# Attention with a gated convolution FFN on one core: q, k and v laid out by the host, masks by a matmul, V's level step folded in, a new order

## The chip, the core and the metric

The program runs on one core of a Trainium2 chip: TensorE (PE, with its weight loads PEld), VectorE (DVE), ScalarE (ACT), GpSimd (POOL) and SyncE (SP), which issues most DMAs. The metric is the device time of one execution in microseconds (us); lower is better.

## The reference

Eight batches, eight heads, 576 positions, head size 64. Block-causal attention (blocks of 64) is followed by an FFN with a convolution of three taps and a gate; the FFN's weights come as float64.

```python
scores = scale * np.matmul(q, k.transpose(0, 1, 3, 2))      # scale = 1/8
scores = np.where(block_i >= block_j, scores, -1000000000.0)
attn = np.exp(scores - np.max(scores, axis=-1, keepdims=True))
attn = attn / (np.sum(attn, axis=-1, keepdims=True) + 1e-09)
x = np.matmul(attn, v)                                       # heads side by side: 576 x 512 a batch
h = np.maximum(x @ w_in, 0.0)                                # 512 -> 1024
conv = sum(conv_w[k] * hp[:, k:k + S, :] for k in range(3))  # hp: h with a zero row at each end
out = h * (1 / (1 + np.exp(-conv))) @ w_out                  # 1024 -> 512
```

## The kernel before

The heads are taken in pairs, two heads of 64 on the 128 partitions, 32 pairs in all. Batch 0 (pairs 0 to 3) is worked in two visits a pair, "A" (queries 0 to 255, `stage_sa`) and "B" (the rest, `stage_sb`), while the weights are loaded, decoded from float64 and split. The 28 pairs of batches 1 to 7 are worked in one visit each (`stage_s`), while PE runs the FFN of the batch before: `ffn` has up projections (L1824), the relu, convolution and gate on ACT, DVE and POOL (L1841 to L1877), and down projections (L1910).

Numbers that need more than one pass of PE are kept as a high and a low part: `qh`, `ql`, `kh`, `kl` for q and k, and three matmuls (high x high and the two mixed products) make a product.

**q and k.** `load_nat` (from L718) loads a pair's q and k with the positions on the partitions, head by head, in rows of 256 bytes, and the last 64 positions by themselves (L731). `naturals` (from L1156) transposes them on PE into a PSUM bank, three 128x128 tiles a group (L1166). For a later pair (`stage_t`) there are three groups, nine transposes. Then ACT writes the high part (L1179, for q with the scale 1/8) and DVE subtracts it from the bank to get the low part (L1182), four pieces each. The last 64 queries of the two heads are also copied to the two corners of a 128x128 tile with zeros elsewhere (`qdh`, `qdl`; ACT L1192, DVE L1195), so that one matmul gives both heads' last scores (L1318). In batch 0 the transposes are L1224 (visit A) and L1166 (visit B), evicted by ACT (L709), and the corners are filled by DMAs (L1244).

**Scores of a later pair.** `stage_s` makes them in three visits (L1391, the two heads on the two halves of the rows). ACT then overwrites the masked 64x64 corners of the bank with -1e9 (L1404, six times a pair), DVE takes the maxima (L1413), ACT the exponentials and their sums (L1416), DVE a reciprocal (L1432, L1436). `two_planes` scales the probabilities into two float16 planes (POOL L1271 or ACT L1273 for the first, DVE L1276 for the second: it reads the probabilities and the first plane, both in SBUF), DMA transposes turn them, and `pair_pv` multiplies them with V (L1781). In batch 0 the mask is a matmul already (L1481, L1542): the identity times a tile of -1e9 on 64 rows, added into the bank.

**V of a later pair.** `load_v` loads it in rows of 256 bytes by four to six issues; ACT sums its magnitudes (L809), PE, DVE and POOL make a power of two of them (L812 to L823), POOL scales V by it (`level`, L829), copies it to float16 (`high`, L704) and subtracts (`low`, L835).

**The order.** The function `order` of the class `Plan` merges the five engines' queues; each operation's place on its engine is set by its number in `TARGETS`. PE is filled up where it would idle with matmuls whose result nobody reads (`work`, L2038). PSUM banks are given out in that order too, eight in all.

## Time and profile before

| | us |
|---|---|
| median of 3 runs | 714.97 |
| lowest, highest | 714.72, 715.11 |
| span of the profiled execution | 711.6 |

The profiled execution's span is 3.4 us under the median of the runs; durations below come from it. The page gives, among others, the busy share of each engine over the span. The trace answers by line, by stretch of time and in order of time. Two neighbouring instructions of an engine overlap at their ends in these records, so that what one costs its queue is read from one start to the next.

### The profile page before, as it was taken

To read this page: it belongs to the slowest core of one execution; us is meant where nothing else is said; L and a number is where in the kernel's file an instruction comes from. 1 tells how busy PE (TensorE), PEld (TensorE's weight loads), DVE (VectorE), ACT (ScalarE), POOL (GpSimd) and SP (SyncE) were. 2 spreads that over 40 slices of the span, in tenths; PEclk is the share of its full clock that TensorE was granted. 3 is DMA by queue.
4 is the path that set the end of the run, shared out by engine and by line. 5 is a ranking of instruction groups with operands and counts; after the bars stand their busy time and mean duration, and the time that the engine had idled before them with its cause. 6 is when DMAs were issued, how large, how long until landed. Compare 5 with 4: busy or idle time off the path is not lost.

```text
span 711.6 us, 17406 instructions
## 1 busy us (share of the span) xinstructions
PE 689.4 (97%) x5824; PEld 575.2 (81%) x5824; DVE 600.5 (84%) x1553; ACT 589.8 (83%) x1859; POOL 476.0 (67%) x716
## 2 busy tenths in 40 slices
PE   8899999998999999999999999999899999999998
PEld 6567778777889788887978888897778879888987
DVE  5999989998888979999988898888998888994441
ACT  6889989897979779798979889997888779884753
POOL 2545285665877758778787758877676767775543
PEclk9999999999999999999999999999999999999999
DMA  8845437699667794957866796877877595574001
GB/s 212 249 101 140 127 63 156 133 184 169 135 133 133 132 178 93 187 111 168 129 133 132 127 183 122 156 143 123 155 125 143 106 192 113 102 141 85 17 29 45
DMA packets 313197, 94.35 MB, mean 133 GB/s; under 512 B 302461, under 2 KB 307605, under 8 KB 313109
## 3 DMA queue, kind: packets, MB, share of 16 engines
q1 hardware_dynamic: 307812, 84.47, 62.1%
q10 hardware_dynamic: 5296, 8.78, 3.8%
q8 instruction: 46, 0.75, 0.4%
q14 instruction: 43, 0.34, 0.2%
HBM read 37.38 MB, written 9.44 MB: 66 GB/s over the span
## 4 chain that ended last, share of the span: by engine, by line
PE 56%; DVE 17%; ACT 16%; issue 3%; POOL 3%; SPq 2%; DMA 2%; ACTq 0%; POOLq 0%; DVEq 0%
PE bank L1910 19%; PE bank L1824 17%; PE bank L1391 5%; PE bank L1781 4%; PE bank L1719 3%; DVE ptbl L1276 3%; DVE su L1413 3%; PE bank L1166 2%; PE bank L1318 2%; ACT t L1864 2%; ACT t L1844 2%; DVE t L1848 2%; ACT bank L1841 1%; DVE t L1867 1%; DVE h L1276 1%
## 5 line engine op out<-in xcount | busy, mean ns | idle before, releaser
L1824 PE MATMUL bank<-x,wih 128*128 128x290 f32 (+3 forms) x1024 | 195.0, 302 | 4.0 <-DVE t L1867 1.8
L1824 PEld LDWEIGHTS bank<-x,wih 128*128 128x128 f32 x1024 | 153.6, 188 | 15.2 <-DVE t L1867 4.3
L1877 POOL TENSOR_TENSOR gl<-t,gh 128x289 fp32r<-128x289 f32 (+3 forms) x128 | 107.7, 845 | 43.0 <-ACT gh L1871 36.9
L1910 PE MATMUL bank<-woh,gh 128*128 128x512 f32 (+1 forms) x296 | 120.0, 406 | 0.1
L1910 PE MATMUL bank<-woh,gl 128*128 128x512 f32 (+1 forms) x296 | 114.8, 388 | 0.0
L1910 PE MATMUL bank<-wol,gh 128*128 128x512 f32 (+1 forms) x296 | 114.5, 387 | 0.0
L1824 PE MATMUL bank<-x,wil 128*128 128x290 f32 (+3 forms) x512 | 108.6, 298 | 0.0
L1413 DVE TENSOR_REDUCE su<-bank 128x1 f32<-128x384 f32 (+3 forms) x224 | 101.2, 481 | 6.7 <-ACT bank L1404 5.9
L1848 DVE SCALAR_TENSOR_TENSOR t<-bank,cw,t 128x286 f32<-128x286 f32 (+3 forms) x128 | 65.4, 512 | 21.9 <-ACT t L1844 18.5
L1824 PEld LDWEIGHTS bank<-x,wil 128*128 128x128 f32 x512 | 81.1, 188 | 1.5 <-issue 0.7
L1867 DVE SCALAR_TENSOR_TENSOR t<-t,bank 128x289 f32<-128x289 f32 (+3 forms) x128 | 56.6, 448 | 16.4 <-ACT t L1864 15.1
L1844 ACT ACTIVATE t<-bank,cw 128x287 f32<-128x287 f32 (+3 forms) x128 | 63.6, 499 | 4.7 <-POOL gl L1877 2.2
L1910 PEld LDWEIGHTS bank<-woh,gh 128*128 128x128 f32 x296 | 55.6, 188 | 13.6 <-issue 3.6
L1910 PEld LDWEIGHTS bank<-woh,gl 128*128 128x128 f32 x296 | 55.6, 188 | 12.1
L1864 ACT ACTIVATE t<-t 128x289 f32<-128x289 f32 (+3 forms) x128 | 55.6, 444 | 10.3 <-DVE t L1852 4.8
L1910 PEld LDWEIGHTS bank<-wol,gh 128*128 128x128 f32 x296 | 55.8, 188 | 7.2
L1841 ACT ACTIVATE bank<-bank 128x288 f32<-128x288 f32 (+3 forms) x128 | 51.2, 403 | 9.7 <-PE bank L1824 9.0
L1271 POOL TENSOR_SCALAR ptbl<-p3f,su 128x512 f16<-128x512 f32 x56 | 43.9, 792 | 11.6 <-DVE su L1436 8.3
L1861 POOL TENSOR_TENSOR t<-t,ptah 128x287 f32<-128x287 f32 (+1 forms) x28 | 25.1, 898 | 39.1 <-DVE t L1848 20.9
L1391 PE MATMUL bank<-kh,qh 64*128 64x384 f32 (+3 forms) x224 | 43.7, 375 | 2.8 <-DVE x L1792 1.5
L1276 DVE SCALAR_TENSOR_TENSOR ptbl<-p3f,su,ptbl 128x512 f16<-128x512 f32 x56 | 46.0, 829 | 0.1
L1416 ACT ACTIVATE p3f<-bank,su 128x512 f32<-128x512 f32 x56 | 38.2, 684 | 6.8 <-DVE su L1413 6.6
(206 smaller groups left out, 1864.3 us busy)
## 6 DMA issues: line engine op xcount, KB each, us to landing
out_dram<-stage ACTq DMA_DIRECT2D x33, 256.0 KB, 3.4
vn<-in_v_dram SPq DMA_DIRECT2D x58, 128.0 KB, 2.8
qnf<-in_q_dram SPq DMA_DIRECT2D x56, 128.0 KB, 2.7
knf<-in_k_dram SPq DMA_DIRECT2D x56, 128.0 KB, 2.8
x<-in_moe_w_out_dram SPq DMA_DIRECT2D x8, 512.0 KB, 3.7
gh<-in_moe_w_in_dram SPq DMA_DIRECT2D x4, 512.0 KB, 5.5
gl<-in_moe_w_in_dram SPq DMA_DIRECT2D x4, 512.0 KB, 4.3
qtf<-in_k_dram SPq DMA_DIRECT2D x32, 32.0 KB, 2.6
```

Source lines behind the costliest of these rows:

```text
L1271: nc.gpsimd.tensor_scalar(out=hi(), in0=c(tb.ap), scalar1=st.ap[:, col:col + 1], scalar2=0.0, op0=ALU.mult, op1=ALU.add)
L1276: nc.vector.scalar_tensor_tensor(out=lo(), in0=c(tb.ap), scalar=st.ap[:, col:col + 1], in1=hi(), op0=ALU.mult, op1=ALU.subtract)
L1391: nc.tensor.matmul(home[z][hh].ap[:, cols(i)], t[q_].ap[r, 128 * i:128 * i + 128], t[k_].ap[r, 64 + 128 * (3 - i):S], start=(n == 0), stop ...
L1413: nc.vector.tensor_reduce(out=st.ap[:, k:k + 1], in_=sb.ap[:, cols(i)], op=ALU.max, axis=AX.X, negate=True)
L1824: nc.tensor.matmul(fb.ap[:, 0:n2], wt[:, c, fs], xs[c][xi].ap[:, x0:x0 + n2], start=(n + c - c0 == 0), stop=(n + c - c0 == 3 * NCC - 1))
L1841: nc.scalar.activation(out=fb.ap[:, 0:n2], in_=fb.ap[:, 0:n2], func=AF.Relu, scale=0.5 if b == 0 else 2.0 ** -17)
L1844: nc.scalar.activation(out=t.ap[:, 0:no], in_=fb.ap[:, own:own + no], func=AF.Copy, scale=cw[:, NFC + f:NFC + f + 1])
L1848: nc.vector.scalar_tensor_tensor(out=t.ap[:, i0:no], in0=fb.ap[:, own + i0 - 1:own + no - 1], scalar=cw[:, f:f + 1], in1=t.ap[:, i0:no], o ...
L1864: nc.scalar.activation(out=t.ap[:, 0:no], in_=t.ap[:, 0:no], func=AF.Tanh)
L1867: nc.vector.scalar_tensor_tensor(out=t.ap[:, 0:no], in0=t.ap[:, 0:no], scalar=1.0, in1=fb.ap[:, own:own + no], op0=ALU.add, op1=ALU.mult)
L1877: nc.gpsimd.tensor_tensor(out=gbuf[1].ap[:, f, carry:carry + no], in0=t.ap[:, 0:no], in1=gbuf[0].ap[:, f, carry:carry + no], op=ALU.subtract)
L1910: nc.tensor.matmul(fb.ap[:, 0:cut], gbuf[a].ap[:, f, cs], w[:, f, ds], start=(f == 0 and n == 0), stop=(f == NFC - 1 and n == 2))
```

## The change

- The host hands over q and k transposed: a pair's two heads are the 128 rows, the positions the columns. q has 128 columns behind the first 512: the last 64 queries of the first head (rows 0 to 63, zeros below) and those of the second (rows 64 to 127, zeros above), so the corner tile of before comes as columns 512 to 639. k's blocks of batches 1 to 7 come in the order in which `stage_s` takes them. V comes as one row of 640 numbers a partition.
- `load_qk` loads each of q and k with one issue; `load_v` loads V with one.
- The transposes (L1166, L1224), their evictions, the corner copies and their DMAs are gone. A later pair gets its high part by one ACT copy each for q and k, and its low part by one DVE instruction each, from the loaded tile and the high part, written back over the loaded tile (L1051 of the changed kernel). In batch 0 one instruction scales q in place (`scale_q`, on DVE for pair 0 and on POOL otherwise).
- The mask of the later pairs becomes a matmul behind each visit's scores (L1225), as in batch 0.
- V: `level` is gone; `high` scales by the power of two itself (POOL, L759), and `low` becomes a DVE instruction that scales and subtracts (L762).
- `TARGETS` is another list of numbers; which instruction stands where has changed on every engine, throughout the program.

```diff
     def load_v(p, at, part, load_at=None):
...
-            for j in range(2):
-                nc.sync.dma_start(out=vn.ap[:, 0:4, j, :],
-                                  in_=v[b, h0 + j, 0:512, :].rearrange("(c p) d -> p c d", p=P))
-            for r in range(0 if part else 1, 2):
-                nc.sync.dma_start(out=vn.ap[64 * r:64 * r + 64, 4, :, :],
-                                  in_=v[b, h0:h0 + 2, 512:576, :].rearrange("j p d -> p j d"))
+            nc.sync.dma_start(out=vn.ap.rearrange("p c j d -> p (c j d)"), in_=v[b, p % NP])
...
-        def level():
-            nc.gpsimd.tensor_scalar(out=src(), in0=src(), scalar1=sc.ap[:, 2:3], scalar2=0.0, op0=ALU.mult, op1=ALU.add)
-
         def high():
-            pool_copy(piece(0), src())
+            nc.gpsimd.tensor_scalar(out=piece(0), in0=src(), scalar1=sc.ap[:, 2:3], scalar2=0.0, op0=ALU.mult, op1=ALU.add)
 
         def low():
-            nc.gpsimd.tensor_tensor(out=piece(1), in0=src(), in1=piece(0), op=ALU.subtract)
+            nc.vector.scalar_tensor_tensor(out=piece(1), in0=src(), scalar=sc.ap[:, 2:3], in1=piece(0), op0=ALU.mult,
+                                           op1=ALU.subtract)
...
     def stage_t(nat, at):
-        t = {nm: two([P, S], F32R, nm) for nm in ("qh", "ql", "kh", "kl")}
...
+        (xq, lq), (xk, lk) = nat
+        t = {"ql": xq, "kl": xk, "qh": two([P, QW], F32R, "qh"), "kh": two([P, S], F32R, "kh")}
...
+            def ev_hi(hi=hi, lo=lo, scale=scale):
+                nc.scalar.activation(out=hi.ap, in_=lo.ap, func=AF.Copy, scale=scale)
+
+            def ev_lo(hi=hi, lo=lo, scale=scale):
+                nc.vector.scalar_tensor_tensor(out=lo.raw, in0=lo.ap, scalar=scale, in1=hi.ap.bitcast(F32), op0=ALU.mult,
+                                               op1=ALU.subtract)
...
+                    tiles = GROUP[z]
+                    for hh in range(2):
+                        r = slice(64 * hh, 64 * hh + 64)
+                        x = home[z][hh].ap[0:64, 0:128 * len(tiles)].rearrange("p (j c) -> p j c", c=128)[:, :, 64:128]
+                        nc.tensor.matmul(x, rident[r, r], maskt[r, :].unsqueeze(1).broadcast_to([64, len(tiles), 64]), start=False,
+                                         stop=True, skip_group_check=True)
...
-                    def mk(sb=sb, tiles=tiles):
...
-                            nc.scalar.activation(out=x, in_=maskt[0:64, :].unsqueeze(1).broadcast_to([64, len(tiles), 64]), func=AF.Copy)
...
-                        e = pl.op(DVE, c_dve(128 * i + 128), mx, t0 + 0.3 + OSH * hh, deps=[m], bufs=[sb, st])
+                        e = pl.op(DVE, c_dve(128 * i + 128), mx, t0 + 0.3 + OSH * hh, deps=[o], bufs=[sb, st])
...
 TARGETS = """
-3 1 4 5 14 15 0 2 6 7 8 9 13 12 29 30 18 24 24 26 28 39 42 12 33 51 1 1 0 0 20 17 3 3 6 1 4 0 3 2 5 4 5 1 2 3 4 10 8 6
...
```

PE's queue at the scores of a later pair, in the middle of the program. Names: `dg` belongs to V's power of two, `rident` is the identity, `qnr` a loaded q; L1166 are transposes, L1824 (L1650 after) up projections, L1910 (L1736 after) down projections, L1391 (L1219 after) scores, L1225 masks; `kxr`, `qxr` are the low parts in the loaded tiles. Before:

```order
L815 MATMUL bank<-dg,ones 128x128
L1824 MATMUL bank<-x,wih 128x290 x2
L1166 MATMUL bank<-rident,qnr_110 128x128 x3
L1824 MATMUL bank<-x,wil 128x290 x2
L1824 MATMUL bank<-x,wih 128x290 x4
L1391 MATMUL bank<-kh,qh 128x512 x2
L1391 MATMUL bank<-kl,qh 128x512 x2
L1391 MATMUL bank<-kh,ql 128x512 x2
```

After:

```order
L1736 MATMUL bank<-woh,gl 128x512
L1219 MATMUL bank<-kh,qh 128x128 x2
L1219 MATMUL bank<-kxr_114,qh 128x128 x2
L1219 MATMUL bank<-kh,qxr_110 128x128 x2
L1219 MATMUL bank<-kh,qh 128x256 x2
L1219 MATMUL bank<-kxr_114,qh 128x256 x2
L1219 MATMUL bank<-kh,qxr_110 128x256 x2
L1225 MATMUL bank<-maskt,rident 64x2x64 x2
L1219 MATMUL bank<-kh,qh 128x384 x2
L1219 MATMUL bank<-kxr_114,qh 128x384 x2
L1219 MATMUL bank<-kh,qxr_110 128x384 x2
L1225 MATMUL bank<-maskt,rident 64x64 x2
```

The transposes that stood between the FFN's matmuls are gone, and a mask row closes each visit's scores.

DVE's queue in the same part of the program, where the low parts of q and k are made (L1182 before, L1051 after; L1413 and L1239 are maxima, L1276 and L1104 second planes, L1867 and L1693 the gate's product). Before:

```order
L1182 SCALAR_TENSOR_TENSOR ql<-bank,qh 128x384
L1848 SCALAR_TENSOR_TENSOR t<-bank,cw,t 128x286
L1852 SCALAR_TENSOR_TENSOR t<-bank,cw,t 128x287
L1436 RECIPROCAL su_169<-su_169 128x2
L1182 SCALAR_TENSOR_TENSOR kl<-bank,kh 128x192
L1346 TENSOR_REDUCE su_169<-st_161 128x1
L1867 SCALAR_TENSOR_TENSOR t<-t,bank 128x287
L818 TENSOR_REDUCE vs<-bank 128x1
L1182 SCALAR_TENSOR_TENSOR ql<-bank,qh 128x128
L1182 SCALAR_TENSOR_TENSOR kl<-bank,kh 128x384
```

After:

```order
L1104 SCALAR_TENSOR_TENSOR ptbl<-p1f_95,su_155,ptbl 128x2x128
L1051 SCALAR_TENSOR_TENSOR qxr_112<-qxf_111,qh 128x640
L1104 SCALAR_TENSOR_TENSOR ptbl<-p1f_97,su_155,ptbl 128x2x128
L1174 TENSOR_REDUCE su_155<-st_147 128x1
L1258 TENSOR_SCALAR su_155<-su_155 128x3
L1262 RECIPROCAL su_155<-su_155 128x3
L1051 SCALAR_TENSOR_TENSOR kxr_116<-kxf_115,kh 128x576
L1104 SCALAR_TENSOR_TENSOR ptbl<-p2f_101,su_155,ptbl 128x3x128
```

Four short pieces that read a bank, spread among the FFN's instructions, have become two long ones that read `qxf`, `kxf` and `qh`, `kh` in SBUF.

PE's queue at the start of the program (`blank`, `rident` with 512 columns: fillers; `qkr`: q and k of batch 0 as loaded; L1224 transposes, L1538 and L1364 scores, L1542 and L1368 masks). Before:

```order
L2038 MATMUL bank_177<-blank_145 128x512 x10
L1224 MATMUL bank_201<-rident_132,qkr10_124 128x128 x2
L1224 MATMUL bank_208<-rident_132,qkr00_121 128x128 x2
L1224 MATMUL bank_213<-rident_132,qkr01_122 128x128 x2
L1538 MATMUL bank_216<-kh_206,qh_211 128x128
L1538 MATMUL bank_218<-kh_206,qh_211 128x128
L1542 MATMUL bank_216<-maskt_136,rident_132 64x64
L1542 MATMUL bank_218<-maskt_136,rident_132 64x64
```

After:

```order
L1863 MATMUL bank_161<-blank_135 128x512 x8
L1364 MATMUL bank_183<-kh_170,qh_172 128x128
L1364 MATMUL bank_185<-kh_170,qh_172 128x128
L1368 MATMUL bank_183<-maskt_126,rident_122 64x64
L1368 MATMUL bank_185<-maskt_126,rident_122 64x64
L1364 MATMUL bank_183<-kh_170,qh_172 128x256
L1364 MATMUL bank_185<-kh_170,qh_172 128x256
L1368 MATMUL bank_183<-maskt_126,rident_122 64x64
```

The three groups of transposes ahead of the first scores are gone, and two fillers fewer stand ahead of these. In the whole program 39 fillers have become 31.

## Rows read from the trace of the kernel before

**Rows 1.** Page, section 1: busy time of each engine, share of the span, instructions.

```profile
PE 689.4 (97%) x5824; PEld 575.2 (81%) x5824; DVE 600.5 (84%) x1553; ACT 589.8 (83%) x1859; POOL 476.0 (67%) x716
```

**Rows 2.** Busy us (instructions) in stretches: length, then PE, PEld, DVE, ACT, POOL, clock, DMA.

```profile
36.00:114.00 78.00, 77.61 (x503) 57.54 (x504) 72.95 (x187) 70.54 (x211) 39.09 (x57) 1.00 0.48 115
114.00:690.00 576.00, 561.82 (x5037) 480.93 (x5036) 496.11 (x1276) 482.38 (x1544) 414.06 (x619) 1.00 0.70 133
```

**Rows 3.** PE in order of time, from 321.2 us: start, us, engine, line, operation.

```profile
321.27 0.40 PE L1910 MATMUL bank<-wol,gh 128*128 128x512 f32 x1
321.51 0.39 PE L1910 MATMUL bank<-woh,gl 128*128 128x512 f32 x1
321.74 0.22 PE L1166 MATMUL bank<-rident,qnr 128*128 128x128 f32 x1
321.80 0.23 PE L1166 MATMUL bank<-rident,qtr 128*128 128x128 f32 x1
321.86 0.25 PE L1166 MATMUL bank<-rident,knr 128*128 128x128 f32 x1
321.94 0.46 PE L1910 MATMUL bank<-woh,gh 128*128 128x512 f32 x1
322.25 0.39 PE L1910 MATMUL bank<-wol,gh 128*128 128x512 f32 x1
```

**Rows 4.** Groups by line, weight loads: count, busy us, mean ns, idle before, releasers.

```profile
L1166 PEld LDWEIGHTS bank<-rident,qnr 128*128 128x128 f32 x120 | 14.5, 140 | 5.8 <-DVE t L1867 1.2 <-ACT p2f L1416 0.8 <-DVE x L1792 0.8
L1166 PEld LDWEIGHTS bank<-rident,knr 128*128 128x128 f32 x120 | 13.8, 140 | 5.3 <-ACT p2f L1416 1.4 <-DVE x L1792 0.8 <-DVE ql L1182 0.7
```

**Rows 5.** PE in order of time, from the start: fillers and first masks.

```profile
1.06 4.39 PE L2038 MATMUL bank<-blank 128*128 128x512 f32 x10 [1.06 <-DVE st L593]
...
6.89 0.28 PE L1542 MATMUL bank<-maskt,rident 64*64 64x64 f32 x2
7.00 0.68 PE L1538 MATMUL bank<-kh,qh 64*128 64x256 f32 x4
7.33 0.38 PE L1542 MATMUL bank<-maskt,rident 64*64 64x64 f32 x2
7.64 0.71 PE L1224 MATMUL bank<-rident,qkr 128*128 128x128 f32 x6
8.19 1.84 PE L2038 MATMUL bank<-rident 128*128 128x512 f32 x7
```

**Rows 6.** Groups by line, DVE: the low parts of q and k.

```profile
L1182 DVE SCALAR_TENSOR_TENSOR kl<-bank,kh 128x192 fp32r<-128x192 f32 (+1 forms) x56 | 24.9, 448 | 1.1 <-ACT qdh L1192 0.4 <-ACT kh L1179 0.3 <-ACT qh L1179 0.3
L1182 DVE SCALAR_TENSOR_TENSOR ql<-bank,qh 128x384 fp32r<-128x384 f32 (+1 forms) x56 | 23.1, 416 | 0.7 <-ACT qh L1179 0.2
L1195 DVE SCALAR_TENSOR_TENSOR qdl<-bank,qdh 64x64 fp32r<-64x64 f32 x56 | 12.1, 216 | 2.6 <-ACT qdh L1192 1.3 <-ACT kh L1179 0.5
```

**Rows 7.** Groups by line, DVE: second planes, both operands in SBUF.

```profile
L1276 DVE SCALAR_TENSOR_TENSOR ptbl<-p3f,su,ptbl 128x512 f16<-128x512 f32 x56 | 46.0, 829 | 0.1
L1276 DVE SCALAR_TENSOR_TENSOR ptbl<-p1f,su,ptbl 128x256 f16<-128x256 f32 x56 | 32.8, 593 | 2.5 <-ACT ptbl L1273 2.4
```

**Rows 8.** The line L1276 by tile: least, median, longest ns, first and last start.

```profile
L1276 DVE SCALAR_TENSOR_TENSOR ptbl<-p3f,su,ptbl x56: 716/744/1897, 108.8 to 648.1; 128x512 f16<-128x512 f32 x56
```

**Rows 9.** All engines in order of time, from 307.5 us: DVE and POOL.

```profile
307.55 0.49 DVE L1276 SCALAR_TENSOR_TENSOR ptbl<-p1f,su,ptbl 128x256 f16<-128x256 f32 x1
...
308.18 0.80 POOL L829 TENSOR_SCALAR vn<-vn,vs 128x640 f32<-128x640 f32 x1
...
308.26 0.98 DVE L1276 SCALAR_TENSOR_TENSOR ptbl<-p1f,su,ptbl 128x256 f16<-128x256 f32 x1
```

**Rows 10.** Groups by line, ACT and POOL: masks, a copy, V's low part.

```profile
L1404 ACT ACTIVATE bank<-maskt 64x64 f32<-64x64 f32 (+1 forms) x168 | 36.2, 231 | 6.2 <-PE bank L1391 4.4 <-ACT stage L1918 0.7 <-issue 0.5
...
L835 POOL TENSOR_TENSOR vx<-vn,vx 128x640 f16<-128x640 f32 x14 | 20.7, 1476 | 0.8
...
L809 ACT ACTIVATE vx<-vn 128x640 bf16<-128x640 f32 x14 | 10.3, 736 | 0.6 <-PE bank L1781 0.5
```

More of the change, by code (lines that the diff above doesn't have):

```diff
@@ L626 @@
         twins[tag] = []
-        at0 = at if tag == "p2" else at0
         for i in range(cap):
@@ L960, in decode @@
         fin, clamp = [], []
+        tot = sum(n for _, n in parts)
         for j, (words, n) in enumerate(parts):
@@ L975, in s3 @@
                                     op0=ALU.logical_shift_left, op1=ALU.bitwise_and)
-        tot = sum(n for _, n in parts)
         if pool:
@@ new lines, in scale_q, with go, first_t @@
+    def scale_q(x, c, at, dep, eng):
+        def go():
+            (nc.gpsimd if eng == POOL else nc.vector).tensor_scalar(out=x.ap[:, c], in0=x.ap[:, c], scalar1=SCALE, scalar2=0.0,
+                                                                    op0=ALU.mult, op1=ALU.add)
+        n = c.stop - c.start
+        return pl.op(eng, c_pool(n) + 0.03 if eng == POOL else c_dve(n, True), go, at, deps=[dep], bufs=[x], port=True)
+    def first_t(nat, p, at):
+        (xq, lq), (xk, lk) = nat
+        o = scale_q(xq, slice(0, Q1), at, lq, DVE if p == 0 else POOL)
+        return {"q": xq, "k": xk}, ([o, lk],) * 2, []
@@ L1958, in fetch @@
         p, part = visits[i]
-        if part != "A":
-            nat[i] = load_nat(p, at, part)
+        nat[i] = load_qk(p, at, part) if part != "A" else first[0][p]
     def transposes(i, at):
```

242 lines of the change are left out of this document (80 added, 162 removed), and 336 rows, old and new, of the table TARGETS.

## The prediction

> **What bounds the kernel now.** I read the busy line of the page first, then the four stretches, then TensorE's timeline, and only then the other engines. The busy line [rows 1] has PE at 97% of the span and VectorE at 84%, ScalarE 83%, GpSimd 67%. The stretches [rows 2] split that: the first 36 us, with fillers in PE's queue, are another matter (below); from 36 to 114 us PE is busy 77.61 of 78.00 us; from 114 to 690 us, where nearly all the work of the 28 pairs of batches 1 to 7 runs, 561.82 of 576.00 us. The granted clock is 1.00 throughout, the upper of the two levels (2.4 GHz). So from 36 us on, the end is set by how much work stands in PE's queue, with about 14 us of idle time in the long stretch. VectorE is the next: 496.11 of 576.00 us there. Work taken out of PE's queue should come off the time nearly one for one, as long as VectorE keeps up.
>
> **Removed from PE: the transposes of q and k.** Each later pair issues 9 transposes in three groups of three (L1166). The timeline shows one group inside a run of down projections [rows 3]: two successive starts without it are 0.23 to 0.24 us apart (321.27 to 321.51); with it, the start at 321.51 is followed by 321.94 and 322.25, two steps in 0.74 us where 0.46 would be normal. The group costs 0.28 us. 28 pairs x 3 groups x 0.28 = **-23.5 us**, all in PE's own queue. The other end: the weight loads of these transposes sat idle 5.8 and 5.3 us before they could start [rows 4], mostly for a bank or an operand. If no other instruction inherits these waits, the removal is worth 11.1 us more, -34.6 us. I take the bare cost, since the chain behind a removed wait usually stops at the next instruction.
>
> In batch 0, the second visits drop 20 transposes and the first visits 16. At 0.28/3 = 0.094 us each that is **-3.4 us**; only the 20 stand where PE has no filler beside it, so the weak end is -1.9 us.
>
> **Added to PE: the mask as a matmul.** Three pairs of 64-row, 64-column matmuls per later pair (L1225 of the changed kernel), in place of six ScalarE writes. The trace has this kind of pair in the first visits of batch 0 [rows 5]: the mask pair at 6.89 us is followed by the next score matmul at 7.00 us, 0.11 us for the pair. The other pair, at 7.33, has its follower at 7.64, 0.31 us; but there the 256-column scores ahead of it are still running and the next instruction is a full-height transpose, so most of this is not the mask's. 28 x 3 x 0.11 = **+9.2 us**; with 0.31 it would be +26.0 us. I take 0.11, since in the new order a mask pair stands directly behind its score matmuls and often ahead of further score matmuls, as the one at 6.89.
>
> **Fillers.** The program inserts matmuls without use where PE would idle: 39 before, 31 now, two of those saved among the first ten (4.39 us for 10, 0.44 each) and six of the later kind (1.84 us for 7, 0.26 each) [rows 5]. 2 x 0.44 + 6 x 0.26 = **-2.4 us**, or nothing if plain idle time takes their place. That the first scores no longer pass through a transpose and a ScalarE copy is what should shorten this stretch.
>
> **VectorE: fewer pieces, but from SBUF.** Six low-part instructions per pair leave (L1182 and L1195): 24.9 + 23.1 + 12.1 = 60.1 us in all [rows 6]. Three come: the low parts of q (640 columns) and k (576), and V's low part (640), which moves over from GpSimd. All three read two operands from SBUF. The nearest rows are L1276, also two from SBUF: 829 ns at 512 columns and 593 at 256 [rows 7], so 0.92 ns a column and about 0.95 us at 640 and 0.89 at 576. 28 x (0.95 + 0.89 + 0.95) = 78 us: **+18 us** on VectorE. From the median at 512, 744 ns [rows 8], each is 0.085 us shorter: 84 x 0.085 = 7 less, +11 us; the longest of the same row, 1897 ns, shows how far one can stretch. This lies beside PE work: 496.11 + 18 = 514 us in a stretch that shrinks to about 562, 91%. The cover is thin but seen to hold: from 36 to 114 us VectorE is at 72.95 of 78.00 us, 94%, with PE at 99.5% [rows 2]. I put 0 on the path. If the cover is gone, what is late is whatever stands behind such an instruction in VectorE's queue: score maxima (ScalarE's exponentials wait for them, and PE for the banks these free) and the FFN's multiplications, which free the banks of the up projection.
>
> A row speaks against this edit [rows 9]: the L1276 that started at 308.26 us took 0.98 us where its twin at 307.55 took 0.49, and it ended 0.26 us after GpSimd's L829, which began 0.08 us ahead of it, was over. The Trainium skill (SBUF — State Buffer, section "Who interferes with whom") has the rule: a VectorE instruction with two SBUF inputs contends with a GpSimd instruction that reads SBUF, the later one blocked for the whole of the other. By that rule the change moves instructions from a kind that doesn't meet GpSimd to the kind that does; the trace agrees, with 0.98 beside 0.49 us. What it would give here is worked out as the last two rivals.
>
> **ScalarE and GpSimd.** ScalarE loses the mask writes (36.2 us) [rows 10] and six short evictions a pair, and gains two copies of at most 736 ns (as L809, 640 columns): 28 x 1.47 = 41 us. GpSimd loses L829 and L835 (1476 ns), and its copy now also scales. Both were behind PE; on the path 0. It helps that a mask no longer passes through ScalarE between PE and the maxima.
>
> **DMA.** Each load of q, k or v becomes one issue with long rows. From 114 us on loads stand about a pair (576/28 = 20 us) ahead of their use and this is hidden; in the first 36 us it is part of the fillers' term. New is that a load of q or k waits until the scores of two pairs before have been read, since the low part now lies in the loaded tile. Behind it in SyncE's queue stand the loads of V and the DMA transposes of the probabilities, whose readers are the attention's second matmuls. I put 0; a late one would show as PE waiting for a DMA at L1219 or L1607.
>
> **Sum.** 711.6 (profiled span) - 23.5 - 3.4 + 9.2 - 2.4 = 691.5 us. The median of the runs is 714.97, 3.4 us over the span; I keep that difference: 694.9, **forecast 695 us**.
>
> **Rivals.**
> *The waits go too.* The bank or operand waits ahead of the transposes are not inherited, and the three banks a pair that they held come free earlier for the rest. For it: the releasers named there are ScalarE's and VectorE's reads of banks [rows 4], and three bank tenancies a pair less ease those. Against it: VectorE is fuller. 695 - 11 = 684 us.
> *The mask is dear.* Each mask pair costs what the second one in the head shows, +26.0 instead of +9.2: 695 + 17 = 712 us. Then the change hardly does on PE what it says. Against it: that row contains another matmul's end.
> *VectorE and GpSimd collide, in part.* The 84 new instructions meet GpSimd as L1276 does at 308.26, 0.49 us longer. GpSimd, at 414.06 us in the long stretch [rows 2], loses 28 x (0.80 + 1.48) = 64 us, so it is busy 350 of 562 and six in ten meet it: 84 x 0.6 x 0.49 = 25 us more on VectorE, 539 of 562. If a third of it reaches PE, +8: 703 us.
> *The same, so that it ends slower.* A new instruction waits out a whole GpSimd instruction of the long kind (1476 ns is L835) and delays the maxima behind it. The break-even is 20 us over 28 pairs, 0.71 us of PE idle time a pair: it decides once half of one such wait a pair reaches PE. With six tenths reaching it, 695 + 28 x 0.6 x 1.48 = 720 us. Against it: the longest GpSimd instructions are the ones that this change removes.
>
> **Chances.** Forecast 0.52; waits go 0.18; VectorE in part 0.17; mask dear 0.06; slower 0.05; anything else 0.02. From 684 to 707 us should hold 8 in 10: it takes in the first and the third rival and leaves out the other two. About 0.2% (1.4 us) is what a measurement of this kernel can tell from no change. Faster by more than that: 0.92; within: 0.03 (between the dear mask and the slower rival); slower: 0.05.
>
> **What would show it.** In the profile after: no L1166-like group among PE's groups; the mask pairs followed by their successors after about 0.11 us; PE still at 96% or more from 40 to 670 us; VectorE near 91% there, the three new instructions at 0.9 to 1.0 us; two fillers fewer ahead of the first scores. Wrong would be PE's share falling below 95% with waits on VectorE, or a successor of the mask pair that starts 0.3 us late throughout.

## The result and the profile after

| | us |
|---|---|
| before, median of 4 runs | 714.85 |
| after, median of 4 runs | 682.27 |
| lowest, highest of after | 681.34, 683.94 |
| span of the profiled execution of after | 680.3 |
| ratio | 0.9551 (95% interval 0.9531 to 0.9571) |

The kernel is 32.6 us faster. The forecast was 695 us, 20 us faster; the range ended at 684, so the time lies 1.7 us below it. 682 is also below the 684 of the rival "the waits go too"; how far that rival's reason holds is said below. TensorE's clock is not what made the difference: the mean granted clock of the profiled execution is 0.998 before and 0.990 after, with 3.4 us at the lower of the two levels before (from 165.5 us on, a short exception to the forecast's "throughout") and 13.6 us after.

The head of the page of the changed kernel, which answers to [rows 1], shows the span and the busy line:

```profile
span 680.3 us, 16254 instructions
PE 663.0 (97%) x5696; PEld 560.4 (82%) x5696; DVE 603.3 (89%) x1470; ACT 551.9 (81%) x1559; POOL 441.0 (65%) x666
```

PE has 26.4 us less, ScalarE 37.9 us less, GpSimd 35 us less. VectorE has 2.8 us more. PE's share is 97% as before. The stretches answer to [rows 2] (columns as there; the first is as long as before and begins, as before, with the first up projection, which started at 36.07 us before and starts at 27.39 now):

```profile
27.39:105.30 77.91, 76.09 (x475) 54.95 (x476) 76.33 (x190) 70.48 (x193) 43.05 (x60) 0.98 0.34 97
105.30:660.00 554.70, 545.49 (x4994) 474.67 (x4993) 500.60 (x1205) 453.61 (x1293) 375.28 (x566) 0.99 0.67 142
```

VectorE is now busy 90% of the long stretch, and 98% of the one before it. The new instructions on it, by line (count, busy us, mean ns), answer to [rows 6]:

```profile
L1051 DVE SCALAR_TENSOR_TENSOR qxr<-qxf,qh 128x640 fp32r<-128x640 f32 x28 | 25.0, 895 | 0.0
L1051 DVE SCALAR_TENSOR_TENSOR kxr<-kxf,kh 128x576 fp32r<-128x576 f32 x28 | 22.4, 800 | 0.0
L762 DVE SCALAR_TENSOR_TENSOR vv<-vn,vs,vv 128x640 f16<-128x640 f32 x14 | 13.7, 975 | 0.0
L762 DVE SCALAR_TENSOR_TENSOR vx<-vn,vs,vx 128x640 f16<-128x640 f32 x14 | 13.0, 930 | 0.0
```

74.1 us came where 60.1 us left; 0.80 to 0.98 us each, as the prediction sized them.

**Where the time went, in PE's queue.** If each instruction of PE is given the time from its start to the next one's start, the trace from PE's first instruction to its last splits up by kind of work. The sums in us, waits included ("all else" takes in the first visits of batch 0, the products with V and the corner scores):

| kind | before | after | difference |
|---|---|---|---|
| transposes of q and k | 31.1 | 0 | -31.1 |
| up and down projections | 431.6 | 425.0 | -6.6 |
| scores of the later pairs | 71.2 | 63.3 | -7.9 |
| their masks | 0 | 13.7 | +13.7 |
| fillers | 13.5 | 12.5 | -1.0 |
| all else | 159.9 | 161.3 | +1.4 |

Some 4 of the 6.6 us of the projections are the tail of the transposes: of the 79 places where transposes stand in a row, 54 have a projection behind them, and its first step takes 0.07 us longer than is usual for its kind (0.31 us instead of 0.23 in [rows 3]). If the other 25 have the same tail, the transposes held, as an estimate, 31.1 + 79 x 0.07, some 37 us of PE's queue, not the 26.9 of the sum. The 10 us between are, by the bare price that e1_bare confirms below, waits at the transposes, and no other kind of work took them over: all else grew by 1.4 us. Only 2.4 us of them are idle time in PE's own records, which overlap; the weight loads of these transposes show them [rows 4]. One group with a wait, 0.50 us from start to start where the one in [rows 3] has 0.20, in the trace of before (columns as in [rows 3]):

```profile
311.11 0.45 PE L1166 MATMUL bank<-rident,knr 128*128 128x128 f32 x3
311.61 0.57 PE L1781 MATMUL bank<-ptbx,vx 128*64 128x256 f16 x8
```

Scores and masks belong together, since the end of a block of scores is now paid by its mask: +5.8 us instead of +9.2. The head of the program came out near the forecast in its total, not in its parts: the first up projection comes 8.7 us earlier, of which some 5 us are PE work that was only moved behind it (eight products with V, six transposes of probabilities, three products for the weights and one for the convolution's), so some 3.5 us are gained against 2.4 + 1.9. The 26 transposes that stood there held 4.2 us; the fillers there, 28 before and 27 now, hold 10 us as before.

This says where the time was, and not yet why. The timeline of PE at a late pair shows two visits' masks (columns as in [rows 3]):

```profile
300.59 0.28 PE L1219 MATMUL bank<-kh,qxr 64*128 64x256 f32 x2
300.71 0.22 PE L1225 MATMUL bank<-maskt,rident 64*64 64x128 f32 x2
300.86 0.44 PE L1219 MATMUL bank<-kh,qh 64*128 64x384 f32 x2
...
306.52 0.40 PE L1219 MATMUL bank<-kh,qxr 64*128 64x512 f32 x2
306.75 0.20 PE L1225 MATMUL bank<-maskt,rident 64*64 64x64 f32 x2
306.88 0.50 PE L1736 MATMUL bank<-woh,gh 128*128 128x512 f32 x1
```

A mask pair's successor starts 0.13 to 0.15 us behind it, not 0.11, yet a good part of that is the end of the scores, which was paid before by the work behind them; e3_nomask and e4_mask2 below part the two.

### The profile page after: what moved, and what is told of

Read it like the earlier page. It is cut to its first block, busy times and chain, and to the rows that moved or that the text cites. A ratio compares the mean times of both kernels' runs of the same rounds, so it can differ in the third digit from the quotient of the medians.

```text
span 680.3 us, 16254 instructions
## 1 busy us (share of the span) xinstructions
PE 663.0 (97%) x5696; PEld 560.4 (82%) x5696; DVE 603.3 (89%) x1470; ACT 551.9 (81%) x1559; POOL 441.0 (65%) x666
## 4 chain that ended last, share of the span: by engine, by line
PE 31%; DVE 12%; ACT 10%; DMA 4%; issue 1%; POOL 1%; POOLq 0%; DVEq 0%; ACTq 0%
PE bank L1736 15%; PE bank L1650 10%; PE bank L1607 3%; DVE su L1239 3%; DVE ptbl L1104 2%; PE bank L1219 2%; ACT t L1670 1%; DMA vn<-in_v_dram 1%; DVE t L1693 1%; ACT bank L1667 1%; PE bank L1146 1%; DMA ptbx<-ptbl 1%; DVE h L1104 1%; DMA ptbh<-ptbl 1%; DVE t L1674 1%
## 5 line engine op out<-in xcount | busy, mean ns | idle before, releaser
L1650 PE MATMUL bank<-x,wih 128*128 128x290 f32 (+3 forms) x1024 | 192.1, 300 | 2.9 <-DVE t L1693 1.7
L1650 PEld LDWEIGHTS bank<-x,wih 128*128 128x128 f32 x1024 | 154.5, 188 | 13.8 <-DVE t L1693 3.0
L1703 POOL TENSOR_TENSOR gl<-t,gh 128x289 fp32r<-128x289 f32 (+3 forms) x128 | 109.1, 858 | 37.1 <-ACT gh L1697 32.5
L1736 PE MATMUL bank<-woh,gh 128*128 128x512 f32 (+1 forms) x296 | 118.9, 402 | 0.0
L1736 PE MATMUL bank<-woh,gl 128*128 128x512 f32 (+1 forms) x296 | 114.9, 388 | 0.0
L1736 PE MATMUL bank<-wol,gh 128*128 128x512 f32 (+1 forms) x296 | 114.8, 388 | 0.0
L1650 PE MATMUL bank<-x,wil 128*128 128x290 f32 (+3 forms) x512 | 108.0, 297 | 0.0
L1239 DVE TENSOR_REDUCE su<-bank 128x1 f32<-128x384 f32 (+3 forms) x224 | 98.2, 481 | 3.7 <-PE bank L1225 3.4
L1674 DVE SCALAR_TENSOR_TENSOR t<-bank,cw,t 128x289 f32<-128x289 f32 (+3 forms) x128 | 64.8, 511 | 30.3 <-ACT t L1670 28.6
L1650 PEld LDWEIGHTS bank<-x,wil 128*128 128x128 f32 x512 | 81.7, 188 | 1.2 <-issue 0.2
L1670 ACT ACTIVATE t<-bank,cw 128x289 f32<-128x289 f32 (+3 forms) x128 | 63.9, 504 | 7.5 <-POOL gl L1703 6.0
L1736 PEld LDWEIGHTS bank<-woh,gl 128*128 128x128 f32 x296 | 55.9, 189 | 12.2
L1736 PEld LDWEIGHTS bank<-woh,gh 128*128 128x128 f32 x296 | 56.0, 189 | 12.0 <-issue 1.4
L1667 ACT ACTIVATE bank<-bank 128x290 f32<-128x290 f32 (+3 forms) x128 | 51.3, 408 | 14.3 <-PE bank L1650 13.6
L1736 PEld LDWEIGHTS bank<-wol,gh 128*128 128x128 f32 x296 | 56.0, 189 | 7.7
L1693 DVE SCALAR_TENSOR_TENSOR t<-t,bank 128x289 f32<-128x289 f32 (+3 forms) x128 | 55.9, 447 | 6.4 <-ACT t L1690 5.3
L1099 POOL TENSOR_SCALAR ptbl<-p3f,su 128x512 f16<-128x512 f32 x56 | 47.6, 855 | 15.3 <-DVE su L1262 12.6
L1219 PE MATMUL bank<-kh,qh 64*128 64x384 f32 (+3 forms) x224 | 45.9, 398 | 2.2 <-DVE x L1618 1.8
L1104 DVE SCALAR_TENSOR_TENSOR ptbl<-p3f,su,ptbl 128x512 f16<-128x512 f32 x56 | 47.2, 855 | 0.0
```

What stands on the lines that cost most here:

```text
L1099: nc.gpsimd.tensor_scalar(out=hi(), in0=c(tb.ap), scalar1=st.ap[:, col:col + 1], scalar2=0.0, op0=ALU.mult, op1=ALU.add)
L1104: nc.vector.scalar_tensor_tensor(out=lo(), in0=c(tb.ap), scalar=st.ap[:, col:col + 1], in1=hi(), op0=ALU.mult, op1=ALU.subtract)
L1219: nc.tensor.matmul(home[z][hh].ap[:, cols(i)], rounded(t[q_])[r, 128 * i:128 * i + 128], rounded(t[k_])[r, 64 + 128 * (3 - i):S], start=(n ...
L1239: nc.vector.tensor_reduce(out=st.ap[:, k:k + 1], in_=sb.ap[:, cols(i)], op=ALU.max, axis=AX.X, negate=True)
L1650: nc.tensor.matmul(fb.ap[:, 0:n2], wt[:, c, fs], xs[c][xi].ap[:, x0:x0 + n2], start=(n + c - c0 == 0), stop=(n + c - c0 == 3 * NCC - 1))
L1667: nc.scalar.activation(out=fb.ap[:, 0:n2], in_=fb.ap[:, 0:n2], func=AF.Relu, scale=0.5 if b == 0 else 2.0 ** -17)
```

## The experiments

Times are medians. Chips differ a little, so each run is compared by its ratio to the kernel before on its own chip; a difference in us is a difference of ratios times 715. For the changed kernel 0.9544 is taken, between 0.9551 and the 0.9537 of its second run. One ratio is sure to about 0.002 to 0.0035, 1.5 to 2.5 us.

| run | what | median | ratio (interval) | against its base, us |
|---|---|---|---|---|
| e5_again | after, again | 683.13 | 0.9537 (0.9519 to 0.9556) | |
| e1_bare | after + bare transposes | 700.85 | 0.9790 (0.9757 to 0.9822) | +18 |
| e2_bank | after + transposes with banks | 702.03 | 0.9813 (0.9782 to 0.9844) | +19 |
| e8_long | the same, full evictions | 719.63 | 1.0058 (1.0036 to 1.0080) | +37 |
| e3_nomask | after, no masks | 680.54 | 0.9502 (0.9465 to 0.9539) | -3 |
| e4_mask2 | after, masks twice | 682.34 | 0.9538 (0.9505 to 0.9571) | 0 |
| e6_dve | after, V's low part twice | 710.20 | 0.9925 (0.9901 to 0.9948) | +27 |
| e7_act | after + ScalarE's masks | 715.89 | 1.0005 (0.9991 to 1.0019) | +33 |
| e11_a_nolow | after, no low part of V | 675.12 | 0.9437 (0.9413 to 0.9461) | -8 |
| e15_a_oneop | after, low parts of q, k shorter | 677.84 | 0.9480 (0.9457 to 0.9503) | -5 |
| e9_b_notr | before, no transposes | 734.30 | 1.0266 (1.0240 to 1.0292) | +19 |
| e10_b_nomask | before, no masks | 712.65 | 0.9968 (0.9951 to 0.9986) | -2 |
| e13_b_tr1 | before, 1 of 3 transposes | 711.50 | 0.9941 (0.9919 to 0.9963) | -4 |
| e16_b_nocorner | before, no corner copies | 711.14 | 0.9931 (0.9909 to 0.9953) | -5 |
| e17_b_trmask | e13 and e10 together | 707.72 | 0.9902 (0.9880 to 0.9924) | -7 |
| e14_b_combo | e13, e10 and e16 together | 700.22 | 0.9783 (0.9759 to 0.9807) | -15.5 |
| e12_ord_old | after, in the order of before | 732.02 | 1.0230 (1.0206 to 1.0253) | +16 to before |

**The price of the transposes: e1_bare and e2_bank.** Both put 84 groups of three back into the changed kernel. The first writes them into the bank that the up projection behind them overwrites:

```diff
                     def mm(...):
+                        for j in range(3 * bare):
+                            nc.tensor.matmul(fb.ap[:, P * j:P * j + P].bitcast(F32R), ones, rident, start=(j == 0), ...)
                         for c in (c0, c0 + 1):
```

> The changed kernel with 84 groups of three 128x128 transposes put back, as many as the later pairs of the kernel before had, but bare: each group stands at the head of an up-projection group (first six of sixteen in each batch from 1 on, two halves), writes the bank that this group overwrites next, reads operands that are long there, and nobody reads what it writes. It adds PE work and no wait. Theory W (the removed transposes cost 84 x 0.28 = 23.5 us of work and some 11 us of waits for banks and operands, which no other instruction inherited): 682.3 + 23.5 = 706 us. Theory D (a group's own price is 0.42 us, there were no waits): 682.3 + 35 = 717 us. Theory O (the bare price is right and the rest of the gain came from elsewhere, the new order or ScalarE's relief): 706 us too; the next run parts it from W.

The second gives each group its own bank and two readers, and `TARGETS` gets places for these operations; all others keep theirs:

```diff
+            o_ = pl.op(PE, 0.28, extra, at, bufs=[tb])
+            o_ = pl.op(ACT, 0.2, read_a, at, deps=[o_], bufs=[tb])
+            pl.op(DVE, 0.13, read_v, at, deps=[o_], bufs=[tb])
```

> The changed kernel with the same 84 groups of three transposes, but each takes a PSUM bank of its own, from which ScalarE and then VectorE read 64 columns each into a scratch tile before it is free; the groups stand some microseconds ahead of the pair's scores, as in the kernel before. It adds PE's work as the run beside it, and three bank tenancies a pair, with 84 short instructions on ScalarE (about 0.2 us each) and on VectorE (0.13 us). Theory W: PE waits for the banks come back: 706 + some 11 = 717 us. Theory O: the tenancies cost nothing, 706 us.

PE's group of these transposes by line (count, busy, mean ns, idle before), first in e1_bare, then in e2_bank:

```profile
L1650 PE MATMUL bank<-rident,ones 128*128 128x128 f32 x252 | 32.4, 237 | 4.0 <-ACT p2f L1242 1.8 <-DVE t L1696 1.4 <-ACT p3f L1242 0.7
```

```profile
L1129 PE MATMUL bank<-rident,ones 128*128 128x128 f32 x252 | 30.9, 242 | 2.0 <-DVE scr L1136 1.2 <-ACT p4f L1261 0.3 <-ACT p1f L1341 0.3
```

In the bare run the transposes hold 18.7 us from start to start and the up projections 3.6 us more: 22.3 / 84 = 0.27 us a group, the bare price of the sum (0.28). The time rose by 18 of these 22 us, some 6 less than theories W and O had it, and half of what theory D wants, which falls. Banks of their own with short readers cost 2 us more, within the noise of the two ratios (some 3), not 11: theory W, in the form "a transpose's bank costs a wait", falls for such banks, as long as the order has room made for the groups. (In e2_bank the transposes hold 23.8 us of PE's queue, 5 more than bare; most of that is made up for elsewhere in the queue.)

**What else the transposes brought: e8_long.** The same groups, but ScalarE and VectorE read all 384 columns:

```diff
-                nc.scalar.activation(out=scr.ap[:, 0:64], in_=tb.ap[:, 0:64], func=AF.Copy)
+                nc.scalar.activation(out=scr.ap[:, 0:384], in_=tb.ap[:, 0:384], func=AF.Copy)
```

> As the run with a bank for each of the 84 groups of three transposes, but ScalarE copies all 384 columns of the bank and VectorE then reads all 384 columns with two operands, as the evictions of the kernel before did (about 0.46 us on ScalarE and 0.42 on VectorE a group), so the bank is held longer and both engines get some 37 us. If the extra gain of the removal (12 us over the bare price) came from how long the transposes' banks were held and from the load of their evictions: 702 + 12 = 714 us. If it came from the new order alone: 702 us.

37 us, 18 more than with the short readers: the long readers cost as much as PE's own work. Three things differ between the two runs, and they are not parted: ScalarE and VectorE have 23 and 28 us more, a group's bank is held 2.15 us on average instead of 1.32, and the added groups stand at other places in the queues (all other instructions keep theirs). PE does not pay at the transposes, which hold 23.0 us of its queue in the profiled execution (23.8 in e2_bank), but at other work, above all the masks, the fillers and the up projections (6.3, 5.2 and 3.3 us more). This is the first hint that the sum's "0 on the path" for those two engines was wrong.

**VectorE and ScalarE in the changed kernel: e6_dve and e7_act.** The first issues V's low part twice, the second lets ScalarE write the masks once more:

```diff
+            for _ in range(2):
                 nc.vector.scalar_tensor_tensor(out=piece(1), in0=src(), ...)
```

```diff
                         def ex(...):
+                            c1 = cols(i).start + 128
+                            nc.scalar.activation(out=sb.ap[0:64, c1 - 64:c1], in_=maskt[0:64, :], func=AF.Copy)
                             nc.scalar.activation(out=x.ap, ..., func=AF.Exp, ...)
```

> The changed kernel with VectorE's new instruction for V's low part issued twice in a row in each of the 28 later pairs (same result): VectorE gets 28 x 0.88 = 24.6 us more, nothing else changes. My step (VectorE's new work lies beside PE's, 0 on the path): the same time as the changed kernel within 2 us. If VectorE's load is on the path, as in the rival of the collision: up to +24.6 us; a third of it, +8.

> The changed kernel with ScalarE's mask writes put back beside the mask matmuls: ahead of each of the 224 exponentials ScalarE also writes the masked 64x64 corner of its tile (the value that is there already), about 0.2 us each, some 45 us, so that ScalarE is as busy as in the kernel before. My step (ScalarE's relief is off the path): the same as the changed kernel within 2 us. Theory O' (the part of the gain that the bare transposes don't explain came from ScalarE's relief): +10 us or more.

VectorE got 25 us more, and the time rose by 27. ScalarE got 47.5 us, and the time rose by 33, seven tenths of it. ScalarE's added writes stand between a maximum and its exponential, so they also lengthen the way of the scores; the run does not part this from the load. The busy line of e6_dve, from its page, and PE's two groups with the most idle time ahead of them there:

```profile
PE 672.6 (95%) x5696; PEld 563.7 (79%) x5696; DVE 629.0 (88%) x1498; ACT 551.6 (78%) x1559; POOL 444.2 (62%) x666
```

```profile
L1651 PE MATMUL bank<-x,wih 128*128 128x290 f32 (+3 forms) x1024 | 195.9, 304 | 9.7 <-DVE t L1694 4.5 <-ACT p2f L1243 2.0 <-DVE x L1619 1.4
L1220 PE MATMUL bank<-kh,qh 64*128 64x384 f32 (+3 forms) x224 | 45.8, 393 | 6.6 <-DVE x L1619 2.1 <-ACT p4f L1163 1.6 <-ACT p1f L1243 1.3
```

And the busy line of e7_act, with the group of its added writes:

```profile
PE 679.2 (95%) x5696; PEld 564.6 (79%) x5696; DVE 605.2 (85%) x1470; ACT 594.0 (83%) x1783; POOL 438.9 (61%) x666
```

```profile
L1243 ACT ACTIVATE bank<-maskt 64x64 f32<-64x64 f32 x224 | 47.5, 212 | 19.8 <-DVE su L1239 18.5 <-ACT stage L1746 0.5
```

No engine is above 95%, VectorE stands at 88% with 82 us to spare in e6_dve, and still every us put onto it came out at the end. PE pays in good part through the banks: it waits until the gate's product (L1694) or V's product (L1619) on VectorE has read one. In the changed kernel the group that answers to L1651 waits 2.9 us, here 9.7:

```profile
L1650 PE MATMUL bank<-x,wih 128*128 128x290 f32 (+3 forms) x1024 | 192.1, 300 | 2.9 <-DVE t L1693 1.7 <-DVE x L1618 0.6 <-ACT p2f L1242 0.6
```

**The mirror: e11_a_nolow and e15_a_oneop.** The same instruction left out, and the low parts of q and k made by one operand (their values change):

```diff
-            nc.vector.scalar_tensor_tensor(out=piece(1), in0=src(), scalar=sc.ap[:, 2:3], in1=piece(0), ...)
+            pass
```

```diff
-                nc.vector.scalar_tensor_tensor(out=lo.raw, in0=lo.ap, scalar=scale, in1=hi.ap.bitcast(F32), ...)
+                nc.vector.tensor_scalar(out=lo.raw, in0=lo.ap, scalar1=scale * 2.0 ** -12, scalar2=None, op0=ALU.mult)
```

> The changed kernel without VectorE's instruction for V's low part (28 x 0.88 = 24.6 us of VectorE; the low part keeps other numbers). The mirror of the run that issued it twice, which cost 27 us. Theory E (VectorE's work is on the path, us for us): 683 - 25 = 658 us. Theory F (the order is fitted to the durations, so only what comes on top is paid): 683 us, at most 5 less.

> The changed kernel with VectorE's two instructions a pair for the low parts of q and k as plain scalings with one operand in SBUF (other numbers in the low parts), about 0.4 us shorter each as an estimate from the nearest shorter rows: VectorE gets some 20 us less. The mirror in the new order: if VectorE's new instructions cost on the path as the added one did, 683 - 20 = 663 us; if only additions are paid, as the run without V's low part says (24.6 us less gave 8), 683 - 6 = 677 us.

25 us less on VectorE gave 8, and 17 us less (603.6 to 586.9) gave 5: 0.3 us for each, where 25 more had cost 1.1 each. What is added is paid, what is taken away comes back by a third as long as the order stays. A set of queues that are fitted to one another would behave so; that reading is argued, not shown by itself.

**The masks: e3_nomask and e4_mask2.**

```diff
-                        nc.tensor.matmul(x, rident[r, r], maskt[r, :]..., start=False, stop=True, ...)
```

(e4_mask2 has this line twice.)

> The changed kernel without the mask matmuls of the later pairs (168 instructions, 84 pairs of them): the part of the scores that the reference masks is left as it is, all else is done. My term (0.11 us a pair): 682.3 - 9.2 = 673 us. By the changed kernel's trace, where a block of scores with its masks is about 0.07 us a pair longer than one without: 682.3 - 5.9 = 676.4 us. The dear mask (0.31): 656 us.

> The changed kernel with each mask matmul of the later pairs issued twice in a row (84 pairs more). My term (0.11 us a pair): 682.3 + 9.2 = 691.5 us. The trace's 0.07: 688.2 us. The dear mask: 708 us.

-3 and 0 us: 0.11 us a pair is too dear for both runs, and 0.07 for the second. In PE's queue, scores and masks together take 73.7 us without masks instead of 77.0, and 81.2 with masks twice. The first difference, 3.3, agrees with the time; the second, 4.2, does not come out in the time, beyond the noise of some 3 us, and so was made up for elsewhere. The timeline of e4_mask2 shows one such place, where four masks take 0.18 us to the next start, against 0.13 for two at 306.75 above:

```profile
307.38 0.25 PE L1226 MATMUL bank<-maskt,rident 64*64 64x64 f32 x4
307.56 0.50 PE L1737 MATMUL bank<-woh,gh 128*128 128x512 f32 x1
```

So a mask pair is worth 0.04 to 0.05 us of PE's queue, less than half of the 0.11 taken from the head.

**One relief at a time in the old order: e13_b_tr1, e10_b_nomask, e16_b_nocorner, e17_b_trmask, e14_b_combo.** All start from the kernel before and keep its `TARGETS`:

```diff
-            o = group([tr_()] * len(cs), [partial(tr, *x) for x in cs], ...)
+            o = group([tr_()] * len(cs), [partial(tr, *x) for x in (cs if dve is not None else cs[:1])], ...)
```

```diff
-                            nc.scalar.activation(out=x, in_=maskt[0:64, :]..., func=AF.Copy)
```

```diff
-                        nc.scalar.activation(out=hi.ap[r, r], in_=tb.ap[r, P:P + 64], func=AF.Copy, scale=SCALE)
+                        pass
...
-                        nc.vector.scalar_tensor_tensor(out=lo.ap[r, r], in0=tb.ap[r, P:P + 64], ...)
+                        pass
```

> The kernel before, in its own order, with one transpose in each of the 84 groups of the later pairs instead of three; the evictions are the same in number, width and place and read the one transposed tile (its first 64 columns, repeated), so the scores of the later pairs are made from other numbers. PE's relief alone: by the starts in the timeline (0.06 to 0.08 us for each further transpose, some of the tail) 84 x 0.13 to 0.19 = 11 to 16 us of PE's queue. If PE's queue sets the end there, as my prediction had it: 715 - 11 to - 16 = 699 to 704 us. Theory F (the queues are packed to one another, PE's relief is lost to other waits until the order is made anew): 711 us or more.

> The kernel before, in its own order, without ScalarE's mask writes of the later pairs (168 instructions, 36.2 us of ScalarE): that part of the scores stays as it is. My step (ScalarE's relief is worth nothing on the path): 715 us. If ScalarE's relief and the shorter way from the scores to the maxima count by themselves: 715 - 10 to - 25 us. Theory F: a few us at most.

> The kernel before, in its own order, without the corner copies of the later pairs (56 on ScalarE, 56 of 216 ns on VectorE, 12.1 us; the corner tiles stay zero, so the last scores are zero). If they explain what the combined run gave beyond its two measured parts (15 - 3.6 - 2.4 = 9 us): 706 us. If the reliefs help one another: 712 us or more.

> The kernel before, in its own order, with one transpose a group instead of three and without ScalarE's mask writes, the corner copies kept. If the parts add up: 715 - 3.6 - 2.4 = 709 us. If PE's and ScalarE's relief help one another: 704 us or less.

> As the run beside it (one transpose a group in the kernel before), and without ScalarE's mask writes (36.2 us) and without the corner copies (ScalarE about 13 us, VectorE 12.1): relief on PE, ScalarE and VectorE together, in the old order. Sum of the parts by theory F: 2.3 us of the masks, a few more: 707 to 711 us. If the reliefs help one another (one engine's relief is only worth something when the others have theirs): 695 us or less.

PE's relief alone gave 4 us where 11 to 16 were expected. From start to start the transposes hold 21.0 us instead of 31.1, 10 less, and the projections 5.1 us more. The transposes' groups in e13_b_tr1, and below them in the kernel before, show what happened:

```profile
L1172 PE MATMUL bank<-rident,qnr 128*128 128x128 f32 x64 | 14.8, 246 | 2.2 <-DVE t L1873 1.1 <-DVE x L1798 0.3 <-ACT p2f L1422 0.3
L1172 PE MATMUL bank<-rident,knr 128*128 128x128 f32 x36 | 8.6, 258 | 2.1 <-ACT p2f L1422 0.9 <-DVE ql L1188 0.3 <-DVE t L1873 0.3
```

```profile
L1166 PE MATMUL bank<-rident,qnr 128*128 128x128 f32 x120 | 18.9, 242 | 1.3 <-DVE t L1867 0.9 <-ACT p2f L1416 0.2
L1166 PE MATMUL bank<-rident,knr 128*128 128x128 f32 x120 | 19.6, 250 | 1.1 <-ACT p2f L1416 0.4 <-DVE ql L1182 0.3
```

104 transposes still wait 4.3 us as idle time, where 272 waited 2.4 before: PE is there sooner, and the bank is not. ScalarE's masks, 36 us of its time, gave 2; the corner copies, about 12 us each on ScalarE and VectorE, gave 5. The first two together gave 7, the sum of the two. All three gave 15.5, where the parts add up to 11.4. The 4 us beyond the sum are little more than the four intervals together allow (3.1, as a root of squares), so "reliefs help one another" is likely and no more than that. What is shown is that relief of ScalarE and VectorE is worth something without any relief of PE (e16_b_nocorner).

**Transposes out, evictions from SBUF: e9_b_notr.**

```diff
-                    nc.scalar.activation(out=hi.ap[:, k0:k0 + n], in_=tb.ap[:, c0:c0 + n], func=AF.Copy, scale=scale)
+                    nc.scalar.activation(out=hi.ap[:, k0:k0 + n], in_=x[:, at_:at_ + n], func=AF.Copy, scale=scale)
```

(with `x` a slice of `wih`; VectorE's low parts and the corners the same way)

> The kernel before, in its own order, without the 84 groups of transposes of the later pairs: no bank is taken for them, and ScalarE's and VectorE's pieces of q and k (same number, same columns, same places in the queues) read from a weight tile in SBUF instead; so the scores of the later pairs are made from other numbers. Theory W (work and waits of the transposes go, whatever the order): 715 - 35 = 680 us. My term alone (0.28 us a group): 715 - 23.5 = 691 us. Theory F (the queues are packed, so that what PE alone is given back is lost to waits on VectorE and ScalarE until the order is made anew): above 700 us.

Slower by 19 us, with all of the 84 groups gone from PE. VectorE's low parts now read two operands from SBUF:

```profile
L1184 DVE SCALAR_TENSOR_TENSOR kl<-wih,kh 128x192 fp32r<-128x192 f32 (+1 forms) x56 | 34.5, 621 | 0.1
L1184 DVE SCALAR_TENSOR_TENSOR ql<-wih,qh 128x384 fp32r<-128x384 f32 (+1 forms) x56 | 33.9, 610 | 1.0 <-ACT qh L1181 0.7
```

621 and 610 ns where [rows 6] had 448 and 416: 20 us more on VectorE in the same places. GpSimd, whose 716 instructions are the same, is busy 492 us instead of 476. The run mixes PE's relief with the load of VectorE and GpSimd, and so does not price either; it shows that the second outweighs the first in that order.

**The whole change in the old order: e12_ord_old.** Only the numbers in `TARGETS` differ from the changed kernel; the instructions that both kernels have follow one another on every engine as in the kernel before:

```diff
 TARGETS = """
-1 0 5 7 6 9 19 18 11 2 3 24 8 5 9 20 40 59 66 28 40 55 0 16 15 0 1 0 4 2 3 1 2 4 6 7 6 5 3 4 4 3 5 8 10 17 22 6 3 7 26 1 5 14 8 18 31 10 7 7 21 23 27
...
```

> The changed kernel, every part of it, but in the order of the kernel before: each instruction that both kernels have stands in its old place, and the new ones stand where those that they replace stood (loads of q and k later where their buffer is not free before). Theory W (the order is a small part): within 10 us of 683. Theory F (the parts are worth something only with an order made for them): 715 us or more.

16 us slower than the kernel before, 49 slower than the changed kernel with the same instructions. The rows of the fillers, in e12_ord_old and then in the changed kernel:

```profile
L1934 PE MATMUL bank<-rident 128*128 128x512 f32 x191 | 53.6, 402 | 2.6 <-ACT p3f L1313 1.4 <-DVE t L1764 0.5 <-ACT p2f L1393 0.3
L1934 PE MATMUL bank<-blank 128*128 128x512 f32 x8 | 3.8, 649 | 1.1 <-DVE st L603 1.1
```

```profile
L1863 PE MATMUL bank<-rident 128*128 128x512 f32 x23 | 8.0, 457 | 0.0
L1863 PE MATMUL bank<-blank 128*128 128x512 f32 x8 | 3.5, 606 | 1.1 <-DVE st L532 1.1
```

199 fillers against 31: from start to start they hold 57 us instead of 12.5. Fillers are put where the order leaves PE without work, so 45 of the 49 us are such time, made to look busy (PE reads 97% on this run's page as well). The order as it was doesn't fit the parts. What in them it doesn't fit is not shown; by the code, a load of q or k now waits for the scores of two pairs before, and VectorE has long pieces where it had short ones.

## Why the prediction was wrong

- *"I take the bare cost, since the chain behind a removed wait usually stops at the next instruction"* is the step of the sum that failed. The transposes stood in it with 26.9 us; they held some 37 us of PE's queue, and the 10 us of waits among these were inherited by nobody. That is most of the 11 us by which the profiled spans beat the sum (31.3 for 20.1); the mask gave 3.4 (5.8 us for 9.2), and fillers and all else took back 1.4 each. The group of [rows 3], from which the price was read, is one that did not wait.
- *The price of the bare work* was right: 0.27 us a group in e1_bare, 0.28 in the sum. The head of the program came out near in total, with fillers that gave nothing there.
- *"Work taken out of PE's queue should come off the time nearly one for one, as long as VectorE keeps up"* does not hold as a rule. In the old order two fifths came off (e13_b_tr1: 4 of 10 us); in the new one 22 us of added bare work cost 18. PE's 97% [rows 1] was read as a queue full of work. It is also 95% in e6_dve and e7_act, which are 27 and 33 us longer with the same PE work, and 97% in e12_ord_old. The Trainium skill (Perfetto Trace Analysis, section "Identifying the Most-Contended Engine") says that matmul busy time is not a good measure of how close a kernel is to its limit on TensorE, and names the share of peak FLOPs and that of the weight loads instead. The runs bear out the first; the weight loads tell little more here: PEld falls from 82% in the changed kernel to 79% in both, when PE falls from 97 to 95%, and with the 199 fillers of e12_ord_old it reads 81%, as in the kernel before [rows 1].
- *"0 on the path" for VectorE and ScalarE* failed too. Their share, 84 and 83%, was taken as cover. e6_dve shows that work added to VectorE is paid in full, e7_act that work added to ScalarE between maxima and exponentials is paid by seven tenths, and e16_b_nocorner and e10_b_nomask that taken work gives 5 and 2 us by itself. ScalarE's 38 us less were put at nothing.
- *VectorE's load*: the three new instructions were sized rightly, 74 us, but the balance is +2.8 us of busy time, not +18. The exchange itself is +14 (74.1 for 60.1), and the durations of all its instructions add up to 701 us instead of 689; the busy time counts overlaps once. The rival of the collision did not come in its size: the new instructions have 0.80 to 0.98 us on average, near the sum's 0.89 to 0.95, where the rival added 0.29. [rows 9] shows a slowdown rather than a wait for the whole of L829: the 0.98 us instruction ended 0.26 us after it, where a full wait, which the prediction read from this row, would have left the 0.49 us of its twin. What the forecast left out is GpSimd's side. With the same instructions of its own, it is busy 428 us instead of 441 when the low parts of q and k read one operand (e15_a_oneop), 432 without V's low part (e11_a_nolow), and 492 instead of 476 in e9_b_notr; the other runs stay within 4 us of their kernel.
- *The mask* was over-priced: a pair takes 0.04 to 0.05 us of PE's queue (e3_nomask, e4_mask2) instead of 0.11.
- *DMA at 0* was right as far as PE shows it: PE and its weight loads waited 2.3 us for DMAs in the kernel before and never in the changed one.
- *The rival "the waits go too"* had the size, 11 us, and the first half of its reason: the waits at the transposes were not inherited. The second half, that three bank tenancies a pair cost the waits, is not borne out where readers are short (e2_bank: 2 us, within the noise) and not settled where they are long (e8_long). The waits went in an order made for the new set of instructions; in the old order the same instructions are slower than before (e12_ord_old).

So the 32.6 us belong to the parts together with their order. The parts in the old order gain nothing, and the sum of reliefs there, with two thirds of the transposes, is 15.5. What a newly made order would give the kernel before was not run, so the order's own share is not known. How the 12 us beyond the forecast split between ScalarE's relief, the evictions and the better fit stays open too: each run that takes one part away does so in an order that was made with it.

## What to carry to other kernels

Where several engines stand at 80% and more and their queues were ordered together, as here, don't take any of them to be off the path: before an edit is costed at nothing on an engine, add work to that engine and see whether it is paid, and take some away too, since the two can differ (1.1 us for each added here, 0.3 for each taken). Read the price of a removed instruction from all its places, waits included, and not from one that did not wait. A high busy share of PE proves neither that PE is the bound nor that it isn't. Changes of the parts need the order made anew before they are judged; the same edit was 16 us slower than before in the old order and 33 us faster in its own.

## What the runs showed of the hardware

- A VectorE instruction with one operand from a bank in PSUM and one from SBUF took 448 and 416 ns, the same with both from SBUF 621 and 610, beside a GpSimd that is busy two thirds of the time (e9_b_notr against [rows 6]). GpSimd's own instructions then took 492 us together instead of 476.
- Three 128x128 transposes in a row among projections cost PE 0.27 to 0.28 us together, of which some 0.07 us is paid by the step of the projection behind them ([rows 3], e1_bare).
- A pair of 64x64 mask matmuls behind a block of 64-row scores is nearly free, 0.04 to 0.05 us: from start to start the scores take 73.7 us without masks and 63.3 with them, and the masks 13.7, so that most of what the masks hold is the end of the block (e3_nomask, e4_mask2).
